# Four raw-weight loads on GpSimd's queue, and the loads of step 6's queries and keys moved ahead in SyncE's, in a retention and feed-forward kernel

## The chip, the cores and the metric

The kernel runs on one core of one Trainium2 chip. The metric is the device time of one execution in microseconds (us); the median of several runs counts. A profile is one execution recorded by the hardware. The engines are named as the profile names them: PE is TensorE (its weight loads are PEld), DVE is VectorE, ACT is ScalarE, POOL is GpSimd, SP is SyncE, which only issues transfers (DMAs). "SPq", "ACTq" and "POOLq" are the queues of instructions of these engines as far as they wait or issue.

## What is computed

For 4 batches, 8 heads, 768 tokens and heads of 64, a retention layer with a decaying state, and then a feed-forward layer over all 3072 tokens:

```python
gamma = 1.0 - 2.0 ** (-5.0 - np.arange(H))
for t in range(S):
    state = gamma * state + k[t] outer v[t]          # per batch and head, 64 x 64
    y[:, :, t] = q[t] @ state / sqrt(64)
x = y.transpose(0, 2, 1, 3).reshape(3072, 512)
h = x @ w_in                                         # 512 x 2048
out = (h * sigmoid(1.702 * h)) @ w_out               # 2048 x 512
```

q, k and v are float32. The two weight matrices are given in 64-bit floating point, 8 MB each, and are narrowed to float32 on the chip.

## The kernel before, in words

**Retention.** The tokens are cut into chunks of 64. A step j handles chunk j of two batches at once, so there are 12 steps for the first two batches and 12 for the others; `load(j, ...)` (line 143) fetches its q, k and v. Four steps make a block of 512 tokens of x, and the feed-forward layer runs block by block. Steps 0 to 5 (`j < NEW`) fetch q as one DMA and turn q and k on PE. From step 6 on, q and k are each fetched by eight DMAs of 32 partitions (lines 171 to 179, tiles q_sq and k_sq) for a 32x32 transpose on DVE (`turn`, line 294); another copy of k (tile kn_in, four DMAs) and v (v_in, four DMAs) belong to the "v" part of the load (lines 180 to 183). In the kernel before, "q" of a step from 6 on fetches both q and k.

**The weights.** Each of 16 weight blocks w0 to w15 (0 to 7 of w_in, 8 to 15 of w_out) comes in two halves, a and b, of 512 KB, as pairs of 32-bit words (`fetch`, line 199). They land in one of three raw buffers, chosen by this list:

```python
RING = [0, 1, 2, 0, 1, 2, 0, 2, 1, 0, 1, 2, 0, 1, 2, 0]
```

So w4 takes the buffer of w1, w7 that of w5, w8 that of w4, w11 that of w7. A buffer is free again when the narrowing of its last block has read it for the last time. The narrowing (`Narrow`, lines 207 to 258) has six works per block: "abs" (ACT, line 237) and "low" (ACT, line 241) read the raw words, "clip" (DVE, 245), "lift" (DVE, 248), "sign" (DVE, 253, reads the raw words too) and "rest" (DVE, 258) build the float32 weights. w6 is needed by the works that follow "rest6", and so on.

**The products.** The up-projection of the first block runs in plain products (`up0`, PE line 476, closed by a "gate", ACT line 457), and the rest in Strassen-like schemes of seven products: for the first blocks line 559 (`zero`) and line 599 (`seven`), whose differences of inputs and weights are made at lines 500 to 533 and 546, later `up` (line 698); the down-projection is at line 954 (`down`) and line 821 (`down49`). Sums of narrowed weights are saved to DRAM by SP (`seven_keep`, line 538, W1D) and read back for later blocks at lines 906 and 1158 (LATE<-W1D).

**The order of the work.** PE runs its instructions in the order in which the program gives them. For the beginning, until all weights are narrowed, a list of names written out by hand (lines 1105 to 1128) gives the order of the works; a name with "@pool" or "@sp" is issued from that engine's queue, else from its usual one (weights, q and v: SP). Loads of steps below 8 and weight loads are kept in the listed order on their queue; every queue works strictly in order, so what stands behind a waiting DMA waits as well. The names of the list used below: q6, k6, v6 are loads of step 6, w4a and w4b the halves of w4, "gate0.1.7" closes unit "up0.1.7", "seven2.0" is the first product of `seven` for weight pair 2, whose copy (line 604, tile p) must be read before the product after next. "aged" scales the state (POOL, line 423, from step 6 on, with the vector whole_h), "decay" scales k (ACT line 323 up to step 5, POOL line 325 from step 6), "anew" rearranges state, mask and decays for step 6 (lines 1043 to 1053).

Around the change SP's order before is: v4, w5b, w1, w6 and others, v5, w4a, w4b, w7a, w7b, then q6 with k6 (16 DMAs), v6 with its copy of k (8), w8a, q7 with k7 (16), w8b, v7 (8), w11b, w9a, w11a, three stores to W1D, w9b. Hardware DMAs (of SP and ACT) take eight semaphores in turn, so each waits for the landing of the eighth before it; DMAs of POOL have eight of their own.

Of the kernel before, what the change touches and what calls it, by code (L numbers as in the profile page):

```python
# [28 lines left out]
def kernel(  # L29
# [29 lines left out]
    pe, act, dve, pool, sp = nc.tensor, nc.scalar, nc.vector, nc.gpsimd, nc.sync  # L59
# [83 lines left out]
    def load(j, what="qkv", engine=None):  # L143

        b, c = j // NC * 2, j % NC
        rows = slice(c * D, (c + 1) * D)
        keep = send if j < 2 * CB else lambda i: i

        def plain(name, src, tag, bufs, engine=sp):
            t = two.tile([P, H, D], F32, name=name + "_in", tag=tag, bufs=bufs)
            QKV[name, j] = t
            for i in range(2):
                if j < NEW:
                    to, at = t[i * D:(i + 1) * D], src[b + i, :, rows, :].rearrange("h p d -> p h d")
                    for n in range(1 if name == "v" else 2):
                        keep(engine.dma_start(*((to, at) if name == "v" else (to[:, n:H:2], at[:, n * HP:(n + 1) * HP]))))
                else:
                    for r in range(2):  # L160
                        keep(engine.dma_start(t[r * D:(r + 1) * D, i * HP:(i + 1) * HP],  # L161
                                              src[b + i, r * HP:(r + 1) * HP, rows, :].rearrange("h p d -> p h d")))

        if j < NEW:
            if "q" in what:
                QKV["q", j] = t = two.tile([P, H * D], F32, name="q_in", tag="q_sq", bufs=2)
                keep((engine or sp).dma_start(t, q[b:b + 2, :, rows, :].rearrange("i h (k p) d -> (i h) k (p d)", p=8)))
            if "k" in what:
                plain("kn", k, "k_sq" if j in (0, 1, 4, 5) else "o", 2, engine or pool)
        elif "q" in what:  # L170
            for name, src in (("q", q), ("k", k)):
                t = two.tile([P, H, D // C4, C4], F32, name=name + "_sq")
                for r0 in range(0, P, C4):
                    for n in range(D // C4):
                        t0 = c * D + n * C4
                        tc.keep_in_program_order(sp.dma_start(  # L176
                            t[r0:r0 + C4, :, n], src[b + r0 // D, :, t0:t0 + C4, r0 % D:r0 % D + C4]
                            .rearrange("h p d -> p h d")))
                QKV[name, j] = t
        if "v" in what:  # L180
            if j >= NEW and c < NC - 1:
                plain("kn", k, "kn", 1)
            plain("v", v, "v", 2, engine or sp)
# [102 lines left out]
    def turn(j):  # L286

        if j < NEW:
            turn_new(j, 1)
            turn_new(j, 0)  # L290
        else:
            QT[j], KT[j] = home(j, "qT"), home(j, "kT")
            for t, name in ((QT[j], "q"), (KT[j], "k")):
                tc.keep_in_program_order(dve.transpose(
                    t.rearrange("p h t -> p (h t)"), QKV.pop((name, j)).rearrange("p h n d -> p (h n d)")))
        if 2 * CB <= j < NCH - 2:
            load(j + 2, "qk")
# [136 lines left out]
    def step(j, f=None):  # L434
        attend(j, f)
        if j is not None:
            masked(j)
            if j > 2 * CB:
                decay(j)
        if f is not None:  # L440
            c = f % NC
            if c == 0:
                updated(f)
            else:
                by_state(f)
            output(f)
            if 0 < c < NC - 1:
                aged(f)
                updated(f)
        if j is not None and 2 * CB < j < NCH - 1:  # L450
            load(j + 1, "v")
# [587 lines left out]
    def late_loads():  # L1039
        load(2 * CB, "qkv")  # L1040
        load(2 * CB + 1, "qk")
# [63 lines left out]
    for name in """  # L1105
        row@sp k0@act table q0 v0 z5 rows turn_q0 turn_k0 q1 w0b k1@sp w0a mask causal turned_q0
        turned2_q0@dve turned_k0 decay0@pool score0 v1 turn_k1 turn_q1 masked0 gain0 turned_k1 turned_q1 turned2_q1@dve own0 abs0b low0b updated0
        decay1@pool score1 clip0b lift0b sign0b rowd whole q2 k2@sp masked1 abs0a low0a rest0b x0 past1 gain1
        clip0a lift0a sign0a own1 rest0a aged1 turn_k2 turn_q2 w2b w2a state1 updated1 x1 turned_k2 turned_q2 turned2_q2@dve
        v2 q3 k3@sp up0.0.2 score2 abs2 decay2 aged2@dve q4 clip2 lift2 sign2 low2 decay3 w3b w3a  # L1110
        masked2 turn_k3 turn_q3 k4@sp gain2 past2 own2 v3 q5 rest2 k5@sp gate0.0.2 turned_k3 turned_q3 turned2_q3@dve updated2
        state2 score3 decay4 low3 turn_q4 turn_k4 up0.0.3 x2 masked3 gain3 past3 own3 abs3 clip3 lift3 sign3
        turned_q4 turned2_q4@dve rest3 turned_k4 score4 turn_k5 turn_q5 up0.0.6 w1a w5b w1b aged3 updated3 state3 w5a v4
        x3 up0.1.3 turned_q5 turned2_q5@dve gate0.0.3 abs1 low1 abs5 clip1 aged4 lift1 sign1 masked4 own4 gain4 w6a
        rest1 clip5 lift5 gate0.0.6 sign5 up0.0.7 past4 w6b decay5 low5 rest5 updated4 v5 gain5 w4a abs6
        gate0.1.3 turned_k5 clip6 state4 x4 lift6 score5 masked5 w4b abs4 up0.1.7 low6 aged5 gate0.0.7 w7a w7b
        low7 low4 q6 sign6 v6 own5 rest6 past5 seven_4.2 state5 gate0.1.7 seven_6.2 updated5 zero2.0 clip4 up0.1.6
        lift4 sign4 x5 seven_52.2 rest4 turn6 anew decay6 abs7 aged6 up0.1.2 w8a gate0.1.2 clip7 zero_x zero2.1
        score6 past6 q7 w8b v7 zero2.2 masked6 lift7 sign7 gain6 rest7 own6 w11b zero2.3 zero2.4 turn7
        w9a updated6 aged7 gate0.1.6 zero2.5 decay7 zero2.6 state6 w11a seven_4.0 x6 zero0.0 score7 masked7 abs8 clip8  # L1120
        past7 zero0.1 state7 seven_6.0 seven_52.0 lift8 sign8 gain7 own7 x7 seven_x zero0.2 zero0.3 zero0.4 zero0.5 low8
        seven_keep.2 w9b abs9 low11 clip9 rest8 lift9 zero0.6 w10a seven2.0 w10b seven2.1 abs11 clip11 lift11 sign11
        seven_4.1 rest11 seven2.2 abs10 seven2.3 seven2.4 seven_w.1 clip10 lift10 sign9 seven0.0 seven2.5 low10 low9 rest9 sign10
        updated7 rest10 seven_4.3 seven2.6 seven0.1 seven0.2 seven0.3 seven0.4 seven1.0 seven_keep.0 w14b w14a w12b w12a abs12 seven_w.3
        clip12 seven0.5 seven0.6 seven_v.1 lift12 sign12 abs14 clip14 low12 rest12 lift14 sign14 seven1.1 seven1.2 w13a seven1.3
        w13b abs13 low14 seven_v.3 clip13 lift13 seven1.4 sign13 seven3.0 seven1.5 rest14 seven1.6 seven3.1 seven3.2 seven3.3 seven3.4
        w15a seven_keep.3 seven_keep.1 w15b abs15 clip15 lift15 low13 low15 sign15 seven3.5 rest13 seven3.6 rest15 late_loads
    """.split():
        name, *e = name.split("@")
        works[name](*[{"sp": sp, "pool": pool, "act": act, "dve": dve}[x] for x in e])  # L1130
# [109 lines left out]
```

## Time and profile before

| | us |
|---|---|
| median of 3 runs | 650.57 |
| lowest and highest of the 3 | 649.11, 650.80 |
| the profiled execution | 651.44 |
| its span, from first to last instruction | 649.7 |

| engine | busy us | share of the span |
|---|---|---|
| DVE | 435.6 | 67% |
| ACT | 184.4 | 28% |
| POOL | 152.0 | 23% |

How to read the profile: all times are us from the start of the span unless marked ns. A row of the timeline has the start, the length, engine, line and operation, out<-in by the program's tiles, the shape and the count of merged instructions, and in brackets the idle time of the engine before it with what ended it. The recorded end of a PE instruction is modelled, so PE's pace is read from the starts. A product of float32 stands in the trace as two records. The chain that ended last goes back from the last instruction: at each step to what released it. The list of waits has engine, tile and line, "<-" who ended the wait, then the total in us, how many times, and the longest.

### The profile page before, as it was taken

What the parts mean: (1) busy time and instruction counts of PE and PEld (TensorE: products, weight loads), DVE (VectorE), ACT (ScalarE), POOL (GpSimd) and SP (SyncE); (2) the same over time, 40 slices, a digit from 0 to 9 for tenths busy, and PEclk for the clock granted to TensorE, in tenths of its full rate; (3) what the DMA queues carried; (4) which work ended last, traced back from release to release, by engine and by line L of the source; (5) the groups of instructions that cost most, each with busy time, mean ns of one, the idle gap of its engine ahead of it and who ended that gap; (6) DMA issues with size and microseconds to landing.
All of it is one profiled execution on the core that took longest, in us unless ns stands there. A gap on an engine that the chain in (4) does not pass through costs nothing.

```text
span 649.7 us, 15510 instructions
## 1 busy us (share of the span) xinstructions
PE 633.4 (97%) x6543; PEld 578.4 (89%) x6543; DVE 435.6 (67%) x643; ACT 184.4 (28%) x329; POOL 152.0 (23%) x184
## 2 busy tenths in 40 slices
PE   7899999999999998999999999999999999999997
PEld 4788888888889997889999889999888999888997
DVE  2879887979989962438874337985246976145854
ACT  3778237661001102332101333100333110233210
POOL 4000211300612435000645000635300425200000
PEclk9989999999999999999999999999999999999999
DMA  9995587783368875720667730667741354221143
GB/s 198 228 258 161 112 252 214 198 209 57 93 200 264 206 175 171 200 67 4 172 179 213 215 85 1 160 161 189 211 95 49 89 174 143 110 91 49 59 153 98
DMA packets 150710, 96.86 MB, mean 149 GB/s; under 512 B 130512, under 2 KB 135888, under 8 KB 149616
## 3 DMA queue, kind: packets, MB, share of 16 engines
q1 hardware_dynamic: 138048, 42.83, 30.2%
q0 software_dynamic: 8672, 40.00, 19.3%
q10 hardware_dynamic: 3920, 13.04, 5.4%
q8 instruction: 51, 0.84, 0.6%
q14 instruction: 19, 0.16, 0.1%
HBM read 79.18 MB, written 14.94 MB: 145 GB/s over the span
## 4 chain that ended last, share of the span: by engine, by line
PE 83%; DMA 9%; SPq 5%; issue 1%; DVE 1%; ACT 1%; ACTq 0%
PE pq L821 33%; PE px L698 17%; PE pz L698 9%; PE pd L954 7%; PE ph L599 6%; PE py L698 4%; DMA W<-in_moe_w_out_dram 2%; SPq L161 2%; PE pa L339 2%; DMA q_in<-in_q_dram 2%; DMA kn_in<-in_k_dram 2%; DMA LATE<-W1D 1%; SPq L176 1%; PE py L367 1%; PE pa L347 1%; DMA v_in<-in_v_dram 1%
## 5 line engine op out<-in xcount | busy, mean ns | idle before, releaser
L821 PE MATMUL pq<-W,G 128*128 128x128 f32 x840 | 100.3, 276 | 0.0
L821 PEld LDWEIGHTS pq<-W,G 128*128 128x128 f32 x840 | 97.0, 192 | 0.8
L796 POOL DMA_DIRECT2D LATE<-W2D x34 | 18.7, 551 | 260.5 <-PE pq L821 139.8
L821 PE MATMUL pq<-LATE 128*128 128x128 f32 x560 | 74.8, 277 | 0.0
L821 PEld LDWEIGHTS pq<-LATE 128*128 128x128 f32 x560 | 68.2, 192 | 0.6
L698 PE MATMUL px<-X,LATE 128*128 128x256 f32 x256 | 60.6, 380 | 2.2 <-DMA LATE<-W1D 2.2
L698 PE MATMUL px<-X,W1A 128*128 128x256 f32 x256 | 60.5, 379 | 0.0
L698 PEld LDWEIGHTS px<-X,LATE 128*128 128x128 f32 x256 | 48.6, 190 | 9.1 <-issue 2.6
L698 PEld LDWEIGHTS px<-X,W1A 128*128 128x128 f32 x256 | 48.4, 190 | 6.3
L743 DVE TENSOR_TENSOR G<-pz,vv 128x512 f32<-128x512 f32 x16 | 11.1, 692 | 51.5 <-ACT vv L713 51.5
L843 ACT ACTIVATE o<-pq 128x512 f32<-128x512 f32 (+1 forms) x18 | 9.8, 544 | 119.9 <-PE pq L821 94.3
L457 ACT ACTIVATE G<-G 128x512 f32<-128x512 f32 x49 | 30.9, 630 | 43.1 <-DVE G L753 19.7
L821 PE MATMUL pq<-LATE,G 128*128 128x128 f32 x280 | 37.0, 275 | 0.0
L821 PE MATMUL pq<-W,LATE 128*128 128x128 f32 x280 | 37.0, 275 | 0.0
L954 PE MATMUL pd<-W,LATE 128*128 128x256 f32 x160 | 35.1, 380 | 0.0
L821 PEld LDWEIGHTS pq<-W,LATE 128*128 128x128 f32 x280 | 34.1, 192 | 0.0
L821 PEld LDWEIGHTS pq<-LATE,G 128*128 128x128 f32 x280 | 34.1, 192 | 0.0
L954 PEld LDWEIGHTS pd<-W,LATE 128*128 128x128 f32 x160 | 30.4, 190 | 4.1
L683 DVE TENSOR_TENSOR G<-G 128x512 f32<-128x512 f32 (+2 forms) x28 | 15.9, 567 | 23.5 <-ACT G L457 23.5
L810 DVE TENSOR_TENSOR LATE<-G 128x512 f32<-128x512 f32 x35 | 27.6, 789 | 5.0 <-PE pq L821 2.2
L476 PE MATMUL ph<-X,W1A 128*128 128x256 f32 x128 | 30.6, 397 | 0.2 <-DVE X L409 0.2
L698 PE MATMUL pz<-X,W1A 128*128 128x256 f32 x128 | 30.3, 380 | 0.0
(214 smaller groups left out, 1163.5 us busy)
## 6 DMA issues: line engine op xcount, KB each, us to landing
LATE<-W2D POOLq DMA_DIRECT2D x34, 768.0 KB, 5.2
W<-in_moe_w_out_dram SPq DMA_DIRECT2D x12, 512.0 KB, 6.0
LATE<-W1D ACTq DMA_DIRECT2D x4, 1536.0 KB, 9.7
LATE<-W1D POOLq DMA_DIRECT2D x4, 1536.0 KB, 8.9
kn_in<-in_k_dram SPq DMA_DIRECT2D x84, 64.0 KB, 4.8
W<-in_moe_w_in_dram SPq DMA_DIRECT2D x10, 512.0 KB, 4.8
out_dram<-o POOLq DMA_DIRECT2D x20, 256.0 KB, 4.6
q_sq<-in_q_dram SPq DMA_DIRECT2D x144, 32.0 KB, 3.0
```

Source lines behind the costliest of these rows:

```text
L161: keep(engine.dma_start(t[r * D:(r + 1) * D, i * HP:(i + 1) * HP], src[b + i, r * HP:(r + 1) * HP, rows, :].rearrange("h p d -> p h d")))
L339: pe.matmul(PAS[HALF[w], u, 0, s, :], kt[HALF[u], w, s, :], qt[HALF[u], w, s, :], start=True, stop=True)
L457: pin(act.activation(g, h[:, i], AF.Gelu_apprx_sigmoid))
L476: pe.matmul(h[:, ab], w, X[:, 2 * th + c // 2, c % 2, :], start=(ab == 0 and c == 0), stop=(c == 3), skip_group_check=True)
L599: pe.matmul(acc[:, u, :], w, x, start=(start and u == 0 and c == 0), stop=(stop and c == 1), skip_group_check=True)
L683: hold(dve.tensor_sub(q[0][1], q[0][0], q[0][1]))
L698: pe.matmul(acc[:, u, :], w1(2 * d + u, sw)[:, c, :], X[:, sx, c, :], start=(start and u == 0 and c == 0), stop=(stop and c == 1), skip_gr ...
L743: dve.tensor_add(a[3], z, v)
L796: engine.dma_start(c, W2D[i])
L810: dve.tensor_add(d[:, 0], s2, a11)
L821: pe.matmul(p0[:, j, :], a[:, d], w[:, d], start=(new and j == 0 and d == 0), stop=(d == NP // 2 - 1), skip_group_check=True)
L954: pe.matmul(p0[:, n, :], g1(m, p, sa)[:, n * P:(n + 1) * P], W2[:, sb, p, :], start=(new and p == 0 and n == 0), stop=(last and p == NP - ...
```

## The change

It changes two things. The works w4a, w4b, w7a and w7b, fetches of raw weights, get "@pool": POOL issues them instead of SP. And the part "q" of a load from step 6 on no longer fetches k as well: "q" and "k" are separate works now, and q6 and k6 are listed directly behind v5 and behind w4b, ahead of w7 and of everything else that SP issued between; q7 and k7 keep their place.

```diff
-        elif "q" in what:
-            for name, src in (("q", q), ("k", k)):
+        else:
+            for name, src in [(x, y) for x, y in (("q", q), ("k", k)) if x in what]:
...
-        rest1 clip5 lift5 gate0.0.6 sign5 up0.0.7 past4 w6b decay5 low5 rest5 updated4 v5 gain5 w4a abs6
-        gate0.1.3 turned_k5 clip6 state4 x4 lift6 score5 masked5 w4b abs4 up0.1.7 low6 aged5 gate0.0.7 w7a w7b
-        low7 low4 q6 sign6 v6 own5 rest6 past5 seven_4.2 state5 gate0.1.7 seven_6.2 updated5 zero2.0 clip4 up0.1.6
...
-        score6 past6 q7 w8b v7 zero2.2 masked6 lift7 sign7 gain6 rest7 own6 w11b zero2.3 zero2.4 turn7
+        rest1 clip5 lift5 gate0.0.6 sign5 up0.0.7 past4 w6b decay5 low5 rest5 updated4 v5 q6 gain5 w4a@pool
+        abs6 gate0.1.3 turned_k5 clip6 state4 x4 lift6 score5 masked5 w4b@pool k6 abs4 up0.1.7 low6 aged5 gate0.0.7
+        w7a@pool w7b@pool low7 low4 sign6 v6 own5 rest6 past5 seven_4.2 state5 gate0.1.7 seven_6.2 updated5 zero2.0 clip4
...
+        zero2.1 score6 past6 q7 k7 w8b v7 zero2.2 masked6 lift7 sign7 gain6 rest7 own6 w11b zero2.3
```

The remaining lines of the diff are the same names broken into lines at other places. On SP the order becomes v5, q6, k6, v6, w8a and on as before. On POOL, w4a and w4b come behind the loads of "whole" (line 1035), then the copy of the decays (line 1048), w7a and w7b, the load of whole_h (line 1045) and the other works of "anew"; before, whole_h was loaded directly behind "whole". The instructions of PE, DVE and ACT are the same in the same order.

More of the change, by code (lines that the diff above doesn't have):

```diff
@@ L1114 @@
         x3 up0.1.3 turned_q5 turned2_q5@dve gate0.0.3 abs1 low1 abs5 clip1 aged4 lift1 sign1 masked4 own4 gain4 w6a
-        rest1 clip5 lift5 gate0.0.6 sign5 up0.0.7 past4 w6b decay5 low5 rest5 updated4 v5 gain5 w4a abs6
-        gate0.1.3 turned_k5 clip6 state4 x4 lift6 score5 masked5 w4b abs4 up0.1.7 low6 aged5 gate0.0.7 w7a w7b
-        low7 low4 q6 sign6 v6 own5 rest6 past5 seven_4.2 state5 gate0.1.7 seven_6.2 updated5 zero2.0 clip4 up0.1.6
-        lift4 sign4 x5 seven_52.2 rest4 turn6 anew decay6 abs7 aged6 up0.1.2 w8a gate0.1.2 clip7 zero_x zero2.1
@@ L1119 @@
-        score6 past6 q7 w8b v7 zero2.2 masked6 lift7 sign7 gain6 rest7 own6 w11b zero2.3 zero2.4 turn7
[L1120 to L1127, printed above, removed]
+        rest1 clip5 lift5 gate0.0.6 sign5 up0.0.7 past4 w6b decay5 low5 rest5 updated4 v5 q6 gain5 w4a@pool
@@ new lines @@
+        abs6 gate0.1.3 turned_k5 clip6 state4 x4 lift6 score5 masked5 w4b@pool k6 abs4 up0.1.7 low6 aged5 gate0.0.7
+        w7a@pool w7b@pool low7 low4 sign6 v6 own5 rest6 past5 seven_4.2 state5 gate0.1.7 seven_6.2 updated5 zero2.0 clip4
+        up0.1.6 lift4 sign4 x5 seven_52.2 rest4 turn6 anew decay6 abs7 aged6 up0.1.2 w8a gate0.1.2 clip7 zero_x
+        zero2.1 score6 past6 q7 k7 w8b v7 zero2.2 masked6 lift7 sign7 gain6 rest7 own6 w11b zero2.3
+        zero2.4 turn7 w9a updated6 aged7 gate0.1.6 zero2.5 decay7 zero2.6 state6 w11a seven_4.0 x6 zero0.0 score7 masked7
@@ new lines @@
+        abs8 clip8 past7 zero0.1 state7 seven_6.0 seven_52.0 lift8 sign8 gain7 own7 x7 seven_x zero0.2 zero0.3 zero0.4
+        zero0.5 low8 seven_keep.2 w9b abs9 low11 clip9 rest8 lift9 zero0.6 w10a seven2.0 w10b seven2.1 abs11 clip11
+        lift11 sign11 seven_4.1 rest11 seven2.2 abs10 seven2.3 seven2.4 seven_w.1 clip10 lift10 sign9 seven0.0 seven2.5 low10 low9
+        rest9 sign10 updated7 rest10 seven_4.3 seven2.6 seven0.1 seven0.2 seven0.3 seven0.4 seven1.0 seven_keep.0 w14b w14a w12b w12a
@@ L1128 @@
+        abs12 seven_w.3 clip12 seven0.5 seven0.6 seven_v.1 lift12 sign12 abs14 clip14 low12 rest12 lift14 sign14 seven1.1 seven1.2
+        w13a seven1.3 w13b abs13 low14 seven_v.3 clip13 lift13 seven1.4 sign13 seven3.0 seven1.5 rest14 seven1.6 seven3.1 seven3.2
+        seven3.3 seven3.4 w15a seven_keep.3 seven_keep.1 w15b abs15 clip15 lift15 low13 low15 sign15 seven3.5 rest13 seven3.6 rest15
+        late_loads
     """.split():
```

## Prediction, made before the changed kernel was run

> **What bounds the kernel now.** I read the page first: busy shares, and the chain that ended last.
>
> ```profile
> PE 633.4 (97%) x6543; PEld 578.4 (89%) x6543; DVE 435.6 (67%) x643; ACT 184.4 (28%) x329; POOL 152.0 (23%) x184
> PE 83%; DMA 9%; SPq 5%; issue 1%; DVE 1%; ACT 1%; ACTq 0%
> ```
>
> TensorE (PE) is busy 97% of the span and owns 83% of the chain; DMA has 9% and SP's queue (SPq) 5%. So time is gained only where PE stands still. Nothing changes before w4, so I read the chain in order of time from there.
>
> ```profile
> 53.71 0.37 SPq L201
> ...
> 70.31 4.51 DMA W<-in_moe_w_out_dram
> ...
> 89.87 9.48 DMA W<-in_moe_w_out_dram
> ...
> 103.12 7.17 PE ph L599 x32
> ```
>
> From 53.7 to 99.4 us the chain runs through SP's queue: w7 is sent late, the loads of step 6 stand behind it, then w8, step 7, and w9b, whose flight of 9.48 us ends at 99.4. ScalarE (ACT) works off what waited for w9, and PE is released at 103.1. That looks like 45 us ruled by SP. But a chain names one predecessor at each step, not how long anybody stood still. So I asked next who waited for whom between 40 and 104 us, and read PE's own rows.
>
> ```profile
> PE ph L559 <- DVE W L546: 0.5, 1, 0.5
> PE ph L559 <- DVE w L517: 0.2, 1, 0.2
> ```
>
> ```profile
> 63.50 7.07 PE L476 MATMUL ph<-X,W1A 128*128 128x256 f32 x32
> 70.40 1.89 PE L559 MATMUL ph<-X,W1A 128*128 128x256 f32 x8
> ...
> 98.89 3.62 PE L599 MATMUL ph<-W,W1A 128*128 128x256 f32 x16
> 103.12 5.45 PE L599 MATMUL ph<-x,w 128*128 128x256 f32 x24 [0.61 <-ACT p L604]
> ```
>
> PE has three waits there: 0.5, 0.2 and, at 103.12, 0.61 us. Elsewhere it issues almost without a hole: the 32 records from 63.50 to 70.40 are 0.216 us each. Two of the three are for VectorE (DVE); only the one at 103.12 goes back to a load, through ACT. At 0.216 us each the 16 records from 98.89 end at 102.34, and the next starts at 103.12. So **0.78 us** of PE is what the chain through SP costs, and no more.
>
> **The change part by part.**
>
> *SP's queue.*
>
> ```profile
> 42.35 1.63 SPq L158 DMA_DIRECT2D v_in<-in_v_dram  x2
> 49.19 0.89 SPq L201 DMA_DIRECT2D W<-in_moe_w_in_dram  x2
> ...
> 54.84 4.74 SPq L176 DMA_DIRECT2D q_sq<-in_q_dram  x8
> SPq L201 <- DVE G L253: 8.7, 2, 5.2
> 48.00:50.00 2.00, 2.00 (x11) 1.77 (x10) 1.97 (x4) 2.00 (x7) 0.00 (x0) 1.00 0.16 25
> ```
>
> The first three are SP's rows (start, length), the fourth its waits for DVE, the last a window whose last two numbers are the DMA engines' share and GB/s. After v5 (out at 43.98) SP stood 5.2 us until sign1 had freed w4's buffer, and 3.6 us (53.71 less 50.08) for sign5 and w7's: together the 8.7 of the list. The change takes off SP both waits and four issues of some 0.45 us, so q6 can start at 44.0 instead of 54.84. Before, q6, k6, kn6 and v6 took from 54.84 to 70.31, so 15.5 us; from 44.0 that ends at 59.5. I take 61: each hardware DMA waits for the eighth before it, and those ahead of q6 are still in flight until about 48, when the engines fall to a share of 0.16. So SP reaches w8a 9 us earlier. There it waits, since w8 reuses w4's raw buffer, until sign4 has read it:
>
> ```profile
> 65.43 1.29 DVE L253 SCALAR_TENSOR_TENSOR G<-W,G 128x512 uint32<-128x512 uint32 x2
> ...
> 76.28 1.30 DVE L253 SCALAR_TENSOR_TENSOR G<-G 128x512 uint32<-128x512 uint32 x2
> ```
>
> sign4 ends at 65.43 + 1.29 = 66.72. So w8a gains 70.31 - 66.75 = **3.6 us**, not 9. What follows on SP (q7, k7, w8b, kn7, v7, w11b, w9a, w11a, three stores of sums, w9b) has one more gate on the way: w11 needs sign7, which ends at 77.6, and w11b would come at about 83. So the row moves up as a whole, w9b's issue from 89.87 to 86.3 and its landing from 99.4 to 95.8.
>
> *What that is worth.*
>
> ```profile
> 97.11 1.13 ACT L241 ACTIVATE W<-W 128x1024 f32<-128x1024 uint32 x1
> 99.38 1.14 ACT L237 ACTIVATE G<-W 128x1024 f32<-128x1024 f32 x1 [1.13 <-DMA W<-in_moe_w_out_dram]
> ...
> 102.47 0.59 ACT L604 ACTIVATE p<-ph 128x512 f32<-128x512 f32 x1
> SPq L176 <- PE ph L599: 5.3, 1, 5.3
> ```
>
> low8 ends at 98.24; abs9 (99.38, after a wait of 1.13 us for w9) then starts at once, ACT is 1.13 us earlier, the copy of p ends at 103.06 - 1.13 = 101.93, ahead of PE's need at 102.34. The whole 0.78 us goes: **-0.78**. What is late next? No load: PE's next wait for a transfer is the one of R2, below, 150 us on. What SP issues later waits for PE again (L176's 5.3 us, at 141), so it moves along with PE. PE's other two waits are DVE's, and DVE is full there:
>
> ```profile
> 49.00:73.00 24.00, 24.00 (x364) 20.43 (x366) 23.44 (x33) 15.62 (x33) 6.18 (x8) 1.00 0.59 152
> ```
>
> It is busy 23.4 of 24 us between 49 and 73, and no wait of DVE for q6 or k6 is in the list. So their earlier arrival earns nothing by itself, and these two waits stay.
>
> *The four loads on GpSimd (POOL).*
>
> ```profile
> 51.22 0.41 POOL L1048 COPY cold<-cold 64x4 f32<-64x4 f32 x1 [36.37 <-ACT G L323]
> ...
> 70.92 1.04 POOL L423 TENSOR_TENSOR state<-state,whole_h 128x512 f32<-128x512 f32 x1
> ...
> 216.07 0.77 POOL L854 DMA_DIRECT2D out_dram<-o  x1 [0.30 <-DMA kn_in<-in_k_dram]
> ```
>
> POOL stood idle for 36.4 us before 51.22. In the new order w4a and w4b stand ahead of that copy, which waits for ACT's decay5 anyway; w7a and w7b behind it, then the load of whole_h, which was issued at the start and is needed at 70.92. Nothing else on POOL is pushed. An issue there costs 0.77 us by L854, which has as many rows (128x2) as these loads. So w4b is issued at 49.2 + 0.75 = 49.95 and handed over at 50.7, w7b at 54.5 and 55.2; on SP they were out at 50.1 and 54.8. Their flight from POOL is not shown; the nearest rows bound it:
>
> ```profile
> LATE<-W2D POOLq DMA_DIRECT2D x34, 768.0 KB, 5.2
> DMA to landing us min/median/max: 3.6/4.6/9.3
> ```
>
> The same loads from SP took 3.6 to 9.3 us, POOL's larger ones (768 KB) 5.2 in the median. I take 5.5 from issue to landing, near the second row, as the engines are nearly free at 48 to 50 and the company is only k6, kn6 and v6: w4b lands at 55.5, w7b at 60. What covers the delay is slack on ACT:
>
> ```profile
> 55.04 1.20 ACT L237 ACTIVATE G<-W 128x1024 f32<-128x1024 f32 x1
> 56.13 1.18 ACT L241 ACTIVATE W1A<-W 128x1024 f32<-128x1024 uint32 x1
> ...
> 59.33 1.16 ACT L241 ACTIVATE W1A<-G 128x1024 f32<-128x1024 uint32 x1 [0.38 <-DMA G<-in_moe_w_in_dram]
> ...
> 61.74 0.36 ACT L457 ACTIVATE g<-ph 128x256 f32<-128x256 f32 x1
> 60.31 1.23 DVE L258 CUSTOM_DVE_ANT_0 W1A<-G,W1A 128x2048 uint16<-128x2048 uint16 x1
> ```
>
> abs4 (55.04) stands ahead of low6, which ends at 57.31 and is needed by DVE's rest6 at 60.31: w4 may come until 55.04 + 3.0 = 58.0. low7 (59.33), low4 and the gate that ends at 62.10 free the PSUM bank of PE's second unit at 63.50 + 16 x 0.216 = 66.95: w7 may come until 64.2. At 5.5 us of flight 2.5 and 4.2 us are left. Cost 0; with that cover gone, a us for each us, since DVE and PE are both full.
>
> **Sum**: -0.78 us. The profiled execution took 651.44 us (span 649.7), 0.87 above the median of the runs shown: 650.66 for it, and 650.57 - 0.78 = **649.8** for the median.
>
> **The rivals.**
>
> *R1, nothing arrives at PE.* If w9b lands no earlier than 97.0 or another wait takes the place of abs9's, the 0.78 shrinks to nothing. For it: 9.48 us of flight, twice the usual 4.6, so the engines and not the issue may set its landing. Against it: what fills the engines is issued by the same SP just before it, and moves up too. 650.6.
>
> *R2, more.* PE's longest wait after 44 us is for a reload of the first weights:
>
> ```profile
> PE px L698 <- DMA LATE<-W1D: 2.2, 1, 2.2
> 247.21 9.70 DMA LATE<-W1D
> ```
>
> ACT's issue at 247.21 stood behind the landing of a load of v, by the semaphores that hardware DMAs share in turn. With four such DMAs fewer, all later ones take another semaphore; if that parted the two, up to 2.2 us would go: 647.6. Against it: the turn shifts by four for every later DMA, so each still waits for the same neighbour.
>
> *R3, slower: GpSimd's descriptor work holds back DVE.* Its place is 49.2 to 55.3, and it decides as soon as DVE loses over 0.78 us there, since DVE has no room before the 0.5 us wait that PE has for it. Rows for both ends:
>
> ```profile
> L774 DVE TENSOR_TENSOR X<-W,X x12: 676/686/1756, 163.6 to 205.7; 128x512 f32<-128x512 f32 x12
> L248 DVE TENSOR_SCALAR X<-X x6: 686/694/845, 106.5 to 146.3; 128x1024 uint32<-128x1024 uint32 x6
> 124.92 1.38 POOL L526 DMA_DIRECT2D w<-W1A  x1 [5.57 <-ACT w L524]
> 125.34 0.84 DVE L248 TENSOR_SCALAR X<-X 128x1024 uint32<-128x1024 uint32 x1
> ```
>
> The first two are groups of DVE (least, median and longest in ns). The longest L774, 2.5 times the median, ran beside a row of subtractions on POOL; the longest L248, 0.84 instead of 0.69 us, beside the POOL issues from 124.92. Four issues of 0.77 us are 3.1: if DVE stood still throughout, +3.1 - 0.78 gives 652.9; at 0.15 each, +0.6 - 0.78 gives 650.4. I take the second as the nearer, being beside an issue too, and as a rival only: none of PE's three waits up to 104 us stands behind such a stretch. The Trainium skill, page "SBUF — State Buffer", section "Who interferes with whom", states the first: GpSimd and a DVE instruction in a two-port mode exclude each other, and whoever comes second waits for the other's whole instruction. The 0.15 us at 125.34 agrees with it in sign, not in size.
>
> *R4, slower: w4 comes after 58.0.* With 9.3 us, the longest flight of these rows, from 49.95: 59.3, so 1.3 us late, and DVE and PE with it: 650.57 - 0.78 + 1.3 = 651.1. Against it: 4.6 is the median, and the engines are free when w4 starts.
>
> **How the numbers follow.** Forecast 0.56; R1 0.17; R2 0.05; R3 0.10, spread from 650.4 to 652.9; R4 0.08; unforeseen 0.04. The forecast is likeliest, so 649.8. The range: down by what the lowest of the three runs lies under their median (650.57 - 649.11 = 1.5), to 648.3; up through R1, R4 and most of R3, to 652.2. It leaves out R2 and the end of R3. 0.3%, about what a measurement of this kernel can tell from no change, is 1.95 us: below 648.6 lies R2 and a little scatter, 0.08; above 652.5 the end of R3 and the unforeseen, 0.11; between, 0.81.
>
> **What would show it.** Right: SP's q6 from 44 us, w8a right behind sign4's end, abs9 without a wait, no idle PE before the row behind p's copy, and all rows from there 0.8 us earlier. Wrong: a wait of rest6 or low7 for a weight load, stretched DVE rows beside POOL's issues at 49 to 55, PE's wait for L546 above 0.5 us, or w9b landing after 97.

## The result, and the profile after

| | before | changed |
|---|---|---|
| median, us | 650.6 | 649.27 |
| lowest and highest, us | 648.5, 655.58 (22 runs) | 646.39, 652.84 (22 runs) |
| the profiled execution, us | 651.44 | 650.35 |
| its span, us | 649.7 | 648.6 |

The ratio of the changed kernel to the one before is 0.997, with a 95% interval of 0.9955 to 0.9984. On 650.6 us that is 1.95 us faster, between 1.0 and 2.9; the two medians alone are 1.33 us apart. The sum of the prediction was 0.78: the sign is right, the time lies in the range, and the gain is larger than the sum. Ratios, here and below, leave out a run that was slow, over 1.5% above the fastest of its kernel (one each in experiments 3, 5 and 6, in 5 the profiled one), while medians hold every run. From the page of the changed kernel, the busy shares and the chain that ended last:

```profile
PE 633.1 (98%) x6543; PEld 578.0 (89%) x6543; DVE 439.7 (68%) x643; ACT 184.2 (28%) x329; POOL 158.0 (24%) x188
PE 78%; DMA 9%; DVE 7%; SPq 2%; ACT 2%; issue 1%; DVEq 0%; ACTq 0%
```

TensorE's share of the span is one point up, and SP's queue has 2% of the chain instead of 5%. The rows of SP in the timeline of the changed kernel:

```profile
45.78 6.96 SPq L176 DMA_DIRECT2D q_sq<-in_q_dram  x8
52.78 6.04 SPq L176 DMA_DIRECT2D k_sq<-in_k_dram  x8
58.87 2.65 SPq L161 DMA_DIRECT2D kn_in<-in_k_dram  x4
...
67.23 0.36 SPq L201 DMA_DIRECT2D W<-in_moe_w_out_dram  x1
...
86.42 0.96 SPq L201 DMA_DIRECT2D W<-in_moe_w_out_dram  x1
```

q6, k6 and the natural keys of step 6 (kn6) go out in the new places, 54.84 has become 45.78 for q6, and w8a and w9b follow at 67.23 and 86.42 (70.31 and 89.87 before). The rows of ACT and of PE, where that arrives:

```profile
56.97 1.17 ACT L237 ACTIVATE G<-W 128x1024 f32<-128x1024 f32 x1 [1.45 <-DMA W<-in_moe_w_in_dram]
...
62.90 1.17 ACT L241 ACTIVATE W1A<-G 128x1024 f32<-128x1024 uint32 x1 [2.05 <-DMA G<-in_moe_w_in_dram]
...
98.57 1.12 ACT L237 ACTIVATE G<-W 128x1024 f32<-128x1024 f32 x1
...
101.63 0.60 ACT L604 ACTIVATE p<-ph 128x512 f32<-128x512 f32 x1
```

```profile
74.33 1.99 PE L559 MATMUL ph<-W,w 128*128 128x256 f32 x8 [0.55 <-DVE W L546]
...
90.57 5.45 PE L559 MATMUL ph<-W,w 128*128 128x256 f32 x24 [0.21 <-DVE w L517]
...
99.31 3.62 PE L599 MATMUL ph<-W,W1A 128*128 128x256 f32 x16
102.76 5.34 PE L599 MATMUL ph<-x,w 128*128 128x256 f32 x24
```

abs9 (98.57) has no bracket any more: it doesn't wait for w9. PE's 16 records from 99.31 run on into those from 102.76 (3.45 us, 0.216 each) where it stood 0.78 us before. abs4 and low7 (56.97, 62.90) now wait for w4 and w7, the loads that GpSimd issues. PE's two waits for VectorE are still there.

One profile of each kernel doesn't say where another microsecond came from, so the runs below had two questions: is the 0.78 made by SP's queue ahead of w9b and by nothing else, and where is the rest?

### The profile page after: what moved, and what is told of

Same layout as the page of the kernel before. It is cut to its first block, busy times and chain, and to the rows that moved or that the text cites. A ratio compares the mean times of both kernels' runs of the same rounds, so it can differ in the third digit from the quotient of the medians.

```text
span 648.6 us, 15518 instructions
## 1 busy us (share of the span) xinstructions
PE 633.1 (98%) x6543; PEld 578.0 (89%) x6543; DVE 439.7 (68%) x643; ACT 184.2 (28%) x329; POOL 158.0 (24%) x188
## 4 chain that ended last, share of the span: by engine, by line
PE 78%; DMA 9%; DVE 7%; SPq 2%; ACT 2%; issue 1%; DVEq 0%; ACTq 0%
PE pq L821 27%; PE px L698 17%; PE pz L698 9%; PE pd L954 6%; PE ph L599 5%; PE py L698 4%; PE ph L559 3%; DMA kn_in<-in_k_dram 2%; DMA LATE<-W1D 1%; DMA k_sq<-in_k_dram 1%; PE pa L339 1%; DMA W2D<-X 1%; PE py L367 1%; PE pa L347 1%; PE py L599 1%
## 5 line engine op out<-in xcount | busy, mean ns | idle before, releaser
L843 ACT ACTIVATE o<-pq 128x512 f32<-128x512 f32 (+1 forms) x18 | 9.8, 545 | 120.3 <-PE pq L821 120.3
L698 PE MATMUL pz<-X,LATE 128*128 128x256 f32 x128 | 30.2, 379 | 0.0
```

What stands on the lines that cost most here:

```text
L698: pe.matmul(acc[:, u, :], w1(2 * d + u, sw)[:, c, :], X[:, sx, c, :], start=(start and u == 0 and c == 0), stop=(stop and c == 1), skip_gr ...
L843: act.activation(to, y, AF.Copy)
```

## The experiments

A loss is read from PE's starts: the time from one record to the next, less the pace of such records where nothing waits (0.216 us for 128x256, 0.112 for 128x128). Times of medians are of runs beside runs of the kernel before on the same chip.

**1. The four loads on GpSimd, nothing moved.** q6 stays behind w7b.

```diff
- w4a ... w4b ... w7a w7b
+ w4a@pool ... w4b@pool ... w7a@pool w7b@pool
```

> The change's first part alone: w4 and w7 are issued by POOL, q6 with k6 keeps its old place in the list. With w4 and w7 gone from SP nothing stands between v5 and q6 any more, so every queue gets the same order as in the changed kernel. Theory (SP's row moves up once the two waits for raw buffers are off SP): the same as the changed kernel in time (ratio to before 0.9955 to 0.9984) and in trace: no PE wait behind the copy of p, w4b and w7b landing 6 to 7.5 us after their issue. Rival (the listed place of q6 and k6 matters): slower than the changed kernel by 0.78 us or more, with the wait at 103. It is also a second look at the changed kernel's wait for LATE<-W1D (1.0 us in its profile, 2.2 before): if that gain is a lasting one it is 1.0 again, if it is scatter it can be anything from 0 to 3.

649.08 us against 650.6, ratio 0.9978 (0.9962 to 0.9993). On every queue the order comes out as in the changed kernel, so this is the change without the listed move, and its profile is one more execution of the changed order. PE's rows:

```profile
74.33 1.99 PE L559 MATMUL ph<-W,w 128*128 128x256 f32 x8 [1.45 <-DVE W L546]
...
99.30 3.62 PE L599 MATMUL ph<-W,W1A 128*128 128x256 f32 x16
102.75 5.34 PE L599 MATMUL ph<-x,w 128*128 128x256 f32 x24
```

The 0.78 us at 103 is gone here too; the move in the list adds nothing once w4 and w7 have left SP. The wait for L546 is larger, 1.45 us; experiment 10 and the part on flights and cover come back to it. w4b and w7b landed 8.2 us after their issue, not the 6 to 7.5 expected.

**2. The move alone.** The changed kernel with the four loads on SP.

```diff
- v5 q6 ... w4a@pool ... w4b@pool k6 ... w7a@pool w7b@pool
+ v5 q6 ... w4a ... w4b k6 ... w7a w7b
```

> The change's second part alone: SP issues v5, q6, w4a, w4b, k6, w7a, w7b, v6; nothing goes to POOL. Theory (what counts is that SP's waits for sign1 and sign5 are filled with q6 and k6): q6 is out at about 51, w4b lands near 56.5, k6 is out at 57, w7b lands near 62.5, both inside the slack of ACT (58.0 and 64.2), v6 is out at 63.5, w8a goes at sign4's end (66.7); PE's wait behind p is gone, ratio 0.997 to 0.999. Rival (it needs POOL's queue, since w4 and w7 stand behind the small loads): rest6 or the gate of up0.1.7 comes late, PE loses 1 to 4 us, ratio 1.001 to 1.005. No DMA changes from hardware to software, so the turn of the semaphores isn't shifted: if that shift is what shortened the wait for LATE<-W1D, it stands at 2.2 us here.

651.31 us against 650.6, ratio 1.0021 (1.0 to 1.0042). ACT's and PE's rows:

```profile
59.76 1.17 ACT L237 ACTIVATE G<-W 128x1024 f32<-128x1024 f32 x1 [5.44 <-DMA W<-in_moe_w_in_dram]
...
67.53 1.14 ACT L241 ACTIVATE W1A<-G 128x1024 f32<-128x1024 uint32 x1 [3.92 <-DMA G<-in_moe_w_in_dram]
```

```profile
63.29 1.13 PE L559 MATMUL ph<-X,W1A 128*128 128x256 f32 x4 [1.34 <-DVE W1A L258]
...
70.29 3.72 PE L476 MATMUL ph<-X,W1A 128*128 128x256 f32 x16 [2.42 <-ACT g L457]
```

w4 and w7 stand behind q6 on SP, abs4 and low7 wait 5.44 and 3.92 us, and PE loses 1.50 and 2.58 us (its starts) at 63.29 and 70.29. The move needs GpSimd's queue; alone it is no gain. PE waits for no reload at 257 here, though the hardware DMAs are as many as before and keep their semaphores: what R2 proposed isn't needed for that wait to go.

**3. w9 on GpSimd instead.** The kernel before, with w9a and w9b on GpSimd; some late loads of v of step 8 come earlier on SP by it.

```diff
- w9a ... w9b
+ w9a@pool ... w9b@pool
```

> The kernel before with w9a and w9b issued by POOL, and nothing else: SP's row of steps 6 and 7 stays late, only ACT's abs9 gets its data early. Theory (of all that the chain through SP shows, only abs9's wait reaches PE): PE's 0.6 us wait behind p is gone, its 0.5 and 0.2 us waits for DVE stay, the time falls by 0.78 us, ratio 0.998 to 0.9995. Rival (the row of steps 6 and 7 is worth something by itself): w9 alone brings nothing or under half of what the changed kernel brings.

650.74 us against 650.6, ratio 0.9991 (0.9972 to 1.0011): by time it decides nothing. In its trace the loss at 103 is gone, but the waits for L546 and L517 cost 1.06 and 1.01 us instead of 0.68 and 0.40, and 0.45 and 0.39 us are lost later.

**4. w7 behind everything of step 6.** How much cover do the four loads have? All four are on SP again here; the edit is against the changed kernel.

```diff
- w4a@pool ... w4b@pool k6 ... w7a@pool w7b@pool low7 low4 sign6 v6
+ w4a ... w4b k6 ... v6 w7a w7b low7 low4 sign6
```

> SP issues v5, q6, w4a, w4b, k6, v6 and only then w7a, w7b, so w7 is sent at about 62.5 and lands near 67.5, past the bound of 64.2. Theory (beyond the bound each us late is a us of PE): low7 starts at about 67.5, the gate that frees the PSUM bank ends at about 70.3, PE waits 3 us before its second unit of L476 near 67, and with 0.78 gained at 103 the kernel is 2 to 3 us slower than before, ratio 1.002 to 1.006. Rival (ACT's and DVE's slack is larger than read off the rows): no wait of PE there, ratio as in the changed kernel.

658.63 us against 650.6, ratio 1.013 (1.0107 to 1.0154), so 8.4 us instead of 2 to 3. ACT's row of low7, PE's rows behind it, and a window (PE busy, then the other engines; the last three numbers are the granted clock of TensorE, the DMA share and GB/s):

```profile
70.81 1.12 ACT L241 ACTIVATE W1A<-G 128x1024 f32<-128x1024 uint32 x1 [8.75 <-DMA G<-in_moe_w_in_dram]
```

```profile
73.54 6.34 PE L476 MATMUL ph<-X,W1A 128*128 128x256 f32 x16 [6.45 <-ACT g L457]
79.72 1.89 PE L559 MATMUL ph<-X,W1A 128*128 128x256 f32 x8
```

```profile
74.00:78.00 4.00, 4.00 (x11) 3.10 (x11) 3.97 (x6) 1.14 (x1) 0.00 (x0) 0.50 0.78 182
```

low7 starts at 70.81, which is 6.6 us behind the 64.2 that the prediction gave as w7's last moment, and PE loses 6.61: w7's slack was read right, and a us costs a us. On top of it the granted clock is 0.50 until past 78: the 16 records from 73.54 take 6.18 us instead of 3.46, so 2.7 us more. Less the losses at 74 and 103 that vanish behind this, 0.68 and 0.78, it is 7.9. What the expectation had too small was the delay of w7, and it had no price for the clock.

**5 and 6. The reload at 257 us, cut in two on ACT's queue.** The longest loss after 42 us is 2.37 us for LATE<-W1D in the profiled execution of before and 1.16 in that of the changed kernel. Was the rest of the gain there?

```diff
- act.dma_start(LATE[:, 24:48], W1D[1])
+ [act.dma_start(LATE[:, 24 + h:36 + h], W1D[1][:, h:h + 12]) for h in (0, 12)]
```

In the kernel before:

> The kernel before, with the one 128x3072 load of LATE from W1D in line 906 cut into two loads of 128x1536 on the same queue; the matmuls at 257 us (L698) read the first half alone, so their wait for it (2.37 us of lost TensorE time in the profiled execution of before, 1.16 in that of after, none in four other kernels) should be gone in every execution. Theory A, that this wait is a steady cost of the kernel before which the change made smaller, and so the part of the gain beyond the forecast 0.78 us: 1.8 to 2.4 us faster than before (ratio 0.9963 to 0.9972). Theory B, that it is a near tie which the scatter of transfers decides anew in each execution, in every one of these kernels: 0.2 to 1.2 us faster (ratio 0.998 to 0.9997).

In the changed kernel:

> The changed kernel with the same cut of line 906. Theory A: what the change gains besides the wait at 257 us is the 0.78 us of the sum, so this kernel is 0.4 to 1.2 us below the one with the cut alone, and 1.0 to 1.2 us at most below the changed kernel; about 2.6 to 3.2 us below before (ratio 0.995 to 0.996). Theory B: it stands to the cut alone as after to before, 1.0 to 2.9 us below, and 0.2 to 1.2 us below the changed kernel (ratio to before 0.9945 to 0.9975).

661.26 and 660.56 us against 651.09, ratios 1.0123 (1.0075 to 1.0172) and 1.0115 (1.0065 to 1.0165). Both theories missed: the edit made a wait. From the chain of the first of the two, in order of time:

```profile
248.97 6.91 DMA q_sq<-in_q_dram
...
256.03 0.36 ACTq L906
...
256.59 0.61 ACT o L843
...
257.24 3.78 PE px L698 x8
```

The second half shares its semaphore with a load of q that SP had issued at 249.0; ACT holds it until that load has landed, 6.91 us later, and the copy out of PSUM (o, L843), for which PE waits, stands behind it. PE loses 5.86 us here, and 2.27 and 1.39 at the same place of the next two steps (363 and 466 us). As a test of the reload it tells nothing.

**7 and 8. Both kernels once more**, for their profiles.

> The kernel before once more, for its profile. Theory A: TensorE loses 1.8 to 2.9 us again at the first product of step 8 that reads LATE (L698, 255 to 258 us), and 0.6 to 0.8 us again at about 73.9 and 103 us. Theory B: the loss at L698 lies anywhere from 0 to 2.4 us, with the issue of that load 1 to 3 us earlier or later against the products; the losses at 73.9 and 103 us stay.

> The changed kernel once more, for its profile. Theory A: TensorE loses 0.8 to 1.6 us again at the first product of step 8 that reads LATE (L698). Theory B: anywhere from 0 to 2.4 us there. Both: about 0.7 us at 74.3 us, nothing at 103 us, and the first load of the values' weights of the raw block 4 issued by GpSimd near 50 us.

650.7 and 648.73 us. In neither does PE wait at 257: 0 where it was 2.37 and 1.16. That wait is a near tie between a transfer and PE, decided anew each time, as theory B says. But before, run again, isn't 2.37 us faster for it. It lost more elsewhere: 1.23 us at the wait for L546 (0.68 in its first profile) and 0.68 at that for L517 (0.40).

**9. The second half of the reload on GpSimd**, so that no wait is added on ACT; in the kernel before and in the changed one.

```diff
- act.dma_start(LATE[:, 24:48], W1D[1])
+ [e.dma_start(LATE[:, h:h + 12], W1D[1][:, h - 24:h - 12]) for e, h in ((act, 24), (pool, 36))]
```

> The kernel before with line 906's load of LATE[:, 24:48] cut in two, the first half (read by the product at 257 us) issued by ScalarE at the old place and the second (read from 267 us) by GpSimd, so that nothing more than the one old wait stands in ScalarE's order. The first half is 128x1536: the same size landed 4.9 to 5.9 us after its issue with the cut alone, so by 252 to 253 us, ahead of TensorE's arrival at 254.7. Theory A (the wait at 257 us is a steady 2 us of before): 1.8 to 2.4 us faster than before (ratio 0.9963 to 0.9972). Theory B (a near tie that falls either way, 2.37 and 0 us in two executions of before): 0 to 1.2 us faster (ratio 0.998 to 1.0). Both: no loss at L698 at 250 to 260 us, and no wait for ACT o L843 there.

> The changed kernel with the same edit of line 906. Against the edit alone it shows the change without the near tie at 257 us: 0.78 us by the sum of the prediction (0.4 to 1.2), if the rest of the measured gain came from that tie; 1.5 to 2 us if the gain beyond the sum lies in the first 110 us. Against before: theory A 2.6 to 3.2 us faster (ratio 0.995 to 0.996), theory B 0.8 to 2.4 us faster (ratio 0.9963 to 0.9988).

649.74 and 647.82 us against 649.78, ratios 0.9997 (0.998 to 1.0015) and 0.9967 (0.9949 to 0.9985). Neither trace has a loss at 257. Theory A is out: without the tie the kernel before is 0.2 us faster, between 1.3 faster and 1.0 slower. And the change is worth as much without the tie as with it, 649.74 - 647.82 = 1.9 us. So the second microsecond comes, in the main, from elsewhere. PE's losses from 42 to 250 us, in us, none under 0.25 counted (the cut of line 906 begins to act at 247):

| execution | 74 (L546) | 90 (L517) | 103 (p) | 134 (W1A) | 215 (W2D) | sum |
|---|---|---|---|---|---|---|
| before, profiled | 0.68 | 0.40 | 0.78 | 0 | 0 | 1.86 |
| before again | 1.23 | 0.68 | 0.71 | 0 | 0 | 2.62 |
| before, cut on ACT | 0.68 | 1.02 | 0.68 | 0.31 | 0.75 | 3.44 |
| before, half on GpSimd | 1.35 | 0.37 | 0.93 | 0 | 0.77 | 3.42 |
| changed, profiled | 0.73 | 0.39 | 0 | 0.30 | 0 | 1.42 |
| changed again | 0.74 | 0.40 | 0 | 0 | 0 | 1.14 |
| changed, cut on ACT | 0.75 | 0.40 | 0 | 0 | 0 | 1.15 |
| changed, half on GpSimd | 0.50 | 0.40 | 0 | 0 | 0 | 0.90 |
| changed order, experiment 1 | 1.63 | 0.39 | 0 | 0 | 0 | 2.02 |

The means of the sums are 2.84 of four and 1.33 of five: 1.5 us, of which 0.78 lies at 103, 0.1 at 74, 0.2 at 90 and 0.4 at 215; without experiment 1 it would be 1.7, with 0.3 at 74. So few executions give no more than a direction, except for the loss at 103: it is in every execution of before and in none of the changed order. The other losses vary, more in before.

**10. Why L546 varies.** The kernel before, run again: GpSimd's, VectorE's and PE's rows, and behind them the same VectorE row in the first profile of before.

```profile
71.16 1.03 POOL L325 TENSOR_TENSOR G<-kn_in,cold 128x512 f32<-128x512 f32 x1 [1.65 <-DMA kn_in<-in_k_dram]
72.15 1.49 POOL L423 TENSOR_TENSOR state<-state,whole_h 128x512 f32<-128x512 f32 x1
```

```profile
72.66 1.53 DVE L546 TENSOR_TENSOR W<-X 128x512 f32<-128x512 f32 x1
```

```profile
74.97 1.99 PE L559 MATMUL ph<-W,w 128*128 128x256 f32 x8 [1.05 <-DVE W L546]
```

```profile
72.43 0.68 DVE L546 TENSOR_TENSOR W<-X 128x512 f32<-128x512 f32 x1
```

GpSimd waits 1.65 us for kn6, then runs its product of the keys (L325) and that of the state (L423, 72.15 to 73.64); VectorE's first subtraction of L546 beside it takes 1.53 us instead of 0.68, and PE waits 0.55 us longer. In the first profile L423 was over at 71.96, and L546 took 0.68. The work just ahead on VectorE, a clip (L245), met GpSimd there instead and took 1.22 us, against 0.92 in before run again; so the two instructions together lose 0.55 us and not 0.85. In the changed kernel kn6 goes out at 58.87 instead of 64.92, GpSimd no longer waits, and L423 ends at 72.40, ahead of L546 at 72.87:

```profile
67.98 1.44 POOL L1053 COPY state<-state 64x256 f32<-64x256 f32 x2 [1.50 <-DMA state<-state]
69.51 1.89 POOL L325 TENSOR_TENSOR G<-kn_in,cold 128x512 f32<-128x512 f32 x1
71.36 1.04 POOL L423 TENSOR_TENSOR state<-state,whole_h 128x512 f32<-128x512 f32 x1
```

In the twelve traces of before, the changed kernel and experiments 1 to 3, 5 to 9 and 11, L546 took 1.53 where L423 began 0.5 to 0.6 us ahead of it (five times) and 0.68 to 0.69 where it had ended (seven times). In three of the five (before run again, experiment 3 and the first kernel of experiment 9) GpSimd had waited 1.34 to 1.76 us for kn6. In experiments 1 and 2 kn6 had come in time, and GpSimd's own copies of the state (L1053) were late. To make it by hand, GpSimd does the product of line 325 twice for step 6:

```diff
- pin(pool.tensor_mul(KD[j] ...
+ for _ in range(1 + (j == 6)): pin(pool.tensor_mul(KD[j] ...
```

> The changed kernel with one instruction more: GpSimd does its product of step 6's natural keys with the decays (line 325) twice over, into the same tile, so that nothing in the result changes; its state product (L423), which ran 71.36 to 72.40 us in the profiled execution of the changed kernel, starts about 1.04 us later and so runs beside VectorE's first W<-X of L546 (72.87 us there). New theory, that the part of the gain which the prediction's sum left out is VectorE running beside GpSimd: in five traces (one of before again, one with a late second half of W1D, the two loads w9 on GpSimd, all four loads on GpSimd without the move, the move alone) this first L546 took 1.53 us where L423 started 0.4 to 0.5 us ahead of it, and 0.68 where L423 was over. Then it takes 1.53 us here (0.68 after), TensorE loses 1.2 to 1.7 us at about 74.5 us (0.73 after), and the kernel is 0.5 to 0.9 us slower than the changed one, about 0.4 to 1.5 us faster than before (ratio 0.9977 to 0.9994). Rival, that the 1.53 us come from L546's own operands or from the late transfer of the keys: 0.68 us here too, TensorE's loss stays at 0.5 to 0.75 us, and the time is that of the changed kernel (ratio 0.9955 to 0.9984).

649.78 us against 650.55, ratio 0.9985 (0.9968 to 1.0003): by the ratio half of the gain is gone, as the new theory has it, but the interval overlaps that of the changed kernel, so the time doesn't decide. Its rows of GpSimd, VectorE and PE:

```profile
68.75 2.17 POOL L1053 COPY state<-state 64x256 f32<-64x256 f32 x2 [2.04 <-DMA state<-state]
71.01 2.48 POOL L325 TENSOR_TENSOR G<-kn_in,cold 128x512 f32<-128x512 f32 x2
73.45 1.48 POOL L423 TENSOR_TENSOR state<-state,whole_h 128x512 f32<-128x512 f32 x1
```

```profile
72.52 1.52 DVE L546 TENSOR_TENSOR W<-X 128x512 f32<-128x512 f32 x1
74.07 1.41 DVE L546 TENSOR_TENSOR W<-X,W 128x512 f32<-128x512 f32 x1
75.41 0.68 DVE L546 TENSOR_TENSOR W<-X 128x512 f32<-128x512 f32 x1
```

```profile
75.54 1.99 PE L559 MATMUL ph<-W,w 128*128 128x256 f32 x8 [1.46 <-DVE W L546]
```

Two subtractions of L546 are stretched now, to 1.52 and 1.41 us, each beside one of GpSimd's, and the third, alone, is 0.68. PE loses 1.63 us (0.73 in the changed kernel). In this execution the copies (68.75) came late too, as in experiment 1: L325 done once would have ended at 72.04, and L423 behind it would have met the first L546 all the same. So the 0.9 us more is not the edit's alone. What the rows show is the meeting: an L546 that runs beside GpSimd is stretched, whichever product GpSimd does, and the next one, alone, is not. The Trainium skill, page "SBUF — State Buffer", section "Who interferes with whom", says that a VectorE instruction with two inputs in SBUF contends with a GpSimd instruction that reads SBUF. These rows agree and give it a price: 0.85 us for a 128x512 subtraction, and GpSimd's product goes from 1.04 to 1.49 us as well.

The loss at 90 has the same shape one step later. In before run again GpSimd waited 2.58 us for kn7 and ran L325 from 88.24 to 89.28, and the clip beside it took 1.17 us instead of 0.69:

```profile
88.66 1.17 DVE L245 TENSOR_SCALAR G<-G 128x1024 f32<-128x1024 f32 x1 [0.39 <-ACT G L237]
```

In experiments 3 and 5 it took 1.31 and 1.46 beside an L325 that had waited 2.54 and 2.48 us. These are the three executions that lost 0.68 to 1.02 us at 90. Where L325 was over in time, in the first profile of before, in experiment 9 and in all of the changed order, L245 took 0.69 to 0.70 us and PE lost 0.37 to 0.40.

**11. Two of the four loads.** The kernel before, with w7a and w7b alone on GpSimd.

```diff
- w7a w7b
+ w7a@pool w7b@pool
```

> The kernel before with only the two loads w7a and w7b on GpSimd, nothing moved: SyncE issues 1.46 us less (2 x 0.73) ahead of w9b, whose lateness made abs9 wait 1.13 us. By the theory that the loss at 103 us is SyncE's issue time ahead of w9b and nothing else, 1.46 is enough: w9b is issued near 88.4 us, abs9 waits 0, TensorE's 0.78 us at 103 us is gone and the kernel is 0.78 us faster (0.3 to 1.2; ratio 0.998 to 0.9995). By the rival that the whole 3 us of SyncE's four loads is needed because waits further down its queue take back what is freed, abs9 still waits 0.4 us or more and TensorE loses 0.3 to 0.78 us at 103 us.

647.82 us against 649.78, ratio 0.9971 (0.995 to 0.9993). Rows of SP, ACT and PE:

```profile
61.38 2.93 SPq L161 DMA_DIRECT2D kn_in<-in_k_dram  x4
...
86.81 1.24 SPq L201 DMA_DIRECT2D W<-in_moe_w_out_dram  x1
```

```profile
98.16 1.12 ACT L237 ACTIVATE G<-W 128x1024 f32<-128x1024 f32 x1
```

```profile
98.90 3.62 PE L599 MATMUL ph<-W,W1A 128*128 128x256 f32 x16
102.36 5.34 PE L599 MATMUL ph<-x,w 128*128 128x256 f32 x24
```

w9b goes out at 86.81, 3.1 us earlier and not the 1.5 expected. The expectation counted two issues at GpSimd's 0.73 us; on SP the two took 1.08, and what it left out is that SP no longer stands 3.6 us before w7 until sign5 has freed its buffer. w8a leaves at 67.11 here and at 67.23 in the changed kernel, both right behind sign4. abs9 doesn't wait, the 0.78 is gone, kn6 is out at 61.38, and L546 takes 0.68. Two loads do what the change does with four and a move, as far as these intervals tell.

## Why the prediction was right, and where it was not

**The 0.78 us.** Right, and shown: 0.68 to 0.93 in the four executions of the table with SP's old order, nothing in the ten other traces, and two issues with one wait off SP (experiment 11) are enough. R1 is out by the same rows.

**SP's queue.** w8a's gate is sign4, as said: it ends at 67.16, w8a goes out at 67.23. The way there was sized too well. q6 started at 45.78 instead of 44.0, and SP was through with step 6 at 65.2 instead of 61; only 2 us were left before the gate, not 6. w8a gained 3.1 us and not 3.6; without the 0.4 us by which this execution was later from its start, 3.5.

**Flights and cover.** w4b and w7b, issued at 50.82 and 55.39, landed at 56.86 and 62.82: 6.0 and 7.4 us of flight instead of 5.5. Of the cover up to 58.0 and 64.2 only 1.1 and 1.4 us remained, instead of 2.5 and 4.2. So R4 didn't happen in this execution, but it did in experiment 1, which has the same order: w4b was 8.2 us in flight and landed at 58.16, and rest6 stood for low6, which ACT does behind abs4:

```profile
60.50 1.22 DVE L258 CUSTOM_DVE_ANT_0 W1A<-G,W1A 128x2048 uint16<-128x2048 uint16 x1 [0.77 <-ACT W1A L241]
```

PE paid at 74, with 1.63 us instead of 0.73, for this together with the meeting of L546. Of the prediction's signs of being wrong, the wait of rest6 came there; that of low7 (2.05 us for w7, inside the cover) and a wait for L546 above 0.5 us (0.55) came already in the changed kernel. And in the changed kernel with the half on GpSimd w7b flew 9.2 us, and PE stood 0.24 us before its second unit of L476. The flight was mis-sized: 5.7 to 8.2 us for w4b and 7.4 to 9.2 for w7b in the six traces that have the four loads on GpSimd. That the gain held with so little cover is in part luck. Experiments 2 and 4 show what lies behind the edge.

**R3.** Around GpSimd's four issues (1.46 and 1.42 us for two each) and that of whole_h behind them, VectorE is held by 0.07 us at most:

```profile
51.31 0.76 DVE L245 TENSOR_SCALAR G<-G 128x1024 f32<-128x1024 f32 x1
56.00 0.69 DVE L245 TENSOR_SCALAR G<-G 128x1024 f32<-128x1024 f32 x1
```

L245 takes 0.76 us at 51.31, and 0.69 at 56.00 beside the issue of whole_h (56.08 to 56.80). As a price of the issues R3 is out. But its mechanism, VectorE held by GpSimd, is in the kernel with GpSimd's products in the place of its issues, and in most of these traces the change made it smaller.

**R2.** The wait at 257 can go without a turn of the semaphores (experiment 2, and before run again), and taking it off for good was worth 0.2 us, between -1.0 and 1.3.

**The step that failed** is the sentence on q6 and k6: "So their earlier arrival earns nothing by itself, and these two waits stay." It looked for a wait of VectorE or PE for what SP loads, and found none. kn6 and kn7 move up behind q6 and k6, and their consumer is GpSimd, whose wait for them stands in the same list of waits of before (40 to 104 us):

```profile
POOL G L325 <- DMA kn_in<-in_k_dram: 2.4, 2, 1.8
```

GpSimd waited for the keys, ran its products later, and held VectorE just before PE's two waits for it. In the profile of before on which the sum stood, the costlier form of that meeting happened to be absent (L546 at 0.68 us); it was there in another execution of the same kernel. The term was 0. By the table it is 0.2 us at 90 and 0.3 at 74, of which 0.1 is left when experiment 1 with its late w4 is counted. So what the prediction said of 103 us is shown, and the rest of the gain is a mechanism that the rows show with a size that they give only roughly. That 649.27 lies in the range rests in part on the range being 3.9 us wide. The step on what is late next failed in a small thing: "No load" overlooked a reload of W1A at 134, 0.30 us in one execution of the changed kernel and 0.31 in one of before.

**Open.** The loss at 215 us for LATE<-W2D (0.75 and 0.77 in two executions of before, none in the changed kernel) is part of the mean by 0.4 us. Whether the change or the scatter of transfers takes it away wasn't settled. The losses at 74 and 90 were not made to come and go by hand: experiment 10's edit met copies that were late anyway, and no run moves kn6 and kn7 alone. Their link to the keys rests on the rows, GpSimd's wait for them in the five traces where SP had all four loads to issue ahead of step 6 as before (0.57 to 1.76 us for kn6), and none in the changed order.

## What to carry to other kernels

A chain that runs for 45 us through one queue is worth, at that place, what the busiest engine stood still because of it, here 0.78 us, and that reading held in every run. But a single profiled execution shows each near tie with one outcome: before pricing a small change, ask of every load that moves who uses it, engines off the critical path as well, and what they run beside. Two instructions that meet on VectorE and GpSimd (0.55 us here), or a DMA that waits in a computing engine's order (5.9 us), can cost as much as such a change gains, or more.

## What the runs showed of the hardware

**The clock after a pause.** PE's pauses of 2.2 us (before, at 257), 2.42 (experiment 2) and 2.55 (experiment 6, at 358) were followed by records at full pace. After 3.48 (experiment 6), 5.70 (experiment 5) and 6.45 us (experiment 4) the granted clock was 0.50 for 3.4 to 6.1 us of PE's work. For the shortest of these, in the changed kernel with the cut on ACT, PE's first row behind the pause and the two windows behind it:

```profile
253.16 3.04 PE L698 MATMUL px<-X,W1A 128*128 128x256 f32 x8 [3.48 <-ACT o L843]
```

```profile
254.00:256.00 2.00, 2.00 (x7) 1.56 (x6) 0.00 (x0) 0.00 (x0) 1.84 (x3) 0.50 1.00 327
258.00:260.00 2.00, 2.00 (x11) 1.77 (x10) 0.69 (x1) 0.60 (x1) 0.00 (x0) 1.00 0.67 159
```

Here the fall came after PE had resumed: the first records are at full pace, and from 254.3 each takes 0.427 us until 257.3, so that the twelve from 253.16 last 4.4 us instead of 2.6: the wait of 3.48 us cost 1.8 more than its length. The Trainium skill, page "TensorE: Matmul & The Clock Gate", section "Part 1: The HAM clock gate", says that the array goes to half rate after an idle window of some 3.4 us and back after a busy one of that length; these three pauses agree. A pause at 34 us doesn't: PE stands 2.72 us in the first profile of before, and the clock falls there too:

```profile
33.88 0.69 PE L339 MATMUL pa<-G 64*64 64x64 f32 x32 [2.72 <-ACT G L323]
35.00:37.00 2.00, 2.00 (x9) 1.81 (x8) 0.66 (x2) 2.00 (x3) 0.00 (x0) 0.50 0.84 180
```

A pause of 2.68 to 2.72 us at this place was followed by half the clock in nine traces and not in two (experiment 1, with 2.71, and the changed kernel with the half on GpSimd, with 2.69). In the clock records of each trace every stretch at one clock between two changes lasts 3.41 us or a whole multiple of it (3.41, 6.83, 10.24, 215.04). So these traces give no length of pause as an edge. Where a pause falls against that grid may be what decides; no run here tests it.

**A DMA on a computing engine's queue** waits there for the landing of a transfer that it has nothing to do with, if the two share a semaphore: 6.4 us in experiment 5, from the issue of the first half (249.17 to 249.50) to the landing at 255.9. During it ACT, otherwise idle, could not copy a PSUM bank.
